# Zero stores of a decode-attention gradient kernel: their source moved from SBUF to memory, and one of them moved in the queue

## The chip, the cores and the metric

The kernel runs on one core of one Trainium2 chip. The metric is the time of one execution on the device in microseconds; lower is better. Before the change it is 282.77 us, the median of 3 runs (282.73 to 283.42).

## What is computed

The reference is a forward pass and its gradients for one decode step. All tensors are bf16.

```python
def _fwd_reference(A_x, A_k_cache, A_v_cache, A_wq, A_wo, B_x, B_w_gate, B_w_up, B_w_down):
    x = A_x                                   # [4, 1, 512]
    xn = _layernorm(x, axis=-1)
    return x + _A_ref(xn, A_k_cache, A_v_cache, A_wq, A_wo) + _B_ref(xn, B_w_gate, B_w_up, B_w_down)
...
# inside _A_ref: only the last W = 1024 of Sk = 4096 cached positions are used
k = jnp.repeat(k_cache[:, :, Sk - W:, :], rep, axis=1)
v = jnp.repeat(v_cache[:, :, Sk - W:, :], rep, axis=1)
...
_out, _vjp = jax.vjp(_f, A_x, A_k_cache, A_v_cache, A_wq, A_wo, B_w_gate, B_w_up, B_w_down)
return (_out, *_vjp(grad_out))
```

`_A_ref` is attention with 32 query heads and 8 key/value heads of width 128; `_B_ref` is a gated feed-forward layer with 1792 hidden columns. The outputs are the result (out_0) and the gradients of x (out_1), of the two caches (out_2 for K, out_3 for V, each 4 x 8 x 4096 x 128), and of the five weights (out_4 to out_8).

For this change one thing matters: the first 3072 of 4096 positions of each cache have no part in the result, so their gradients are zero, and the kernel has to write these zeros. That is three quarters of out_2 and out_3: 50.3 MB.

## The kernel before

All five engines follow an order written out by hand; the program says what each engine issues and in what sequence, and a framework adds the semaphore waits that the data need.

The kernel loads the feed-forward weights first and computes the feed-forward part. Then it goes through the attention in NT = 4 steps of two key/value heads each (`for t in range(NT)`; in the text the steps are also called groups, so the second group is t = 1). In each step K and V blocks are transposed on TensorE, scores and their softmax are formed, and from them the gradients of V and K (`dvdk`), of wo and wq (`dw`), and partial sums for x. The gradient work is cut into pieces of about one matmul and one copy out of PSUM. Pieces are put in a list, `bg`, and `tick(n)` takes the next n of them, so that they fill the gaps of the following work; most pieces of step t thus run while step t + 1 is under way. When the last piece of an output tile is done, the piece stores it. The tiles are named after what they hold: `stg_dv` and `stg_dk` are gradients of V and K (1 MB each), `osb_o` and `osb_q` gradients of wo and wq (512 KB each), `osb_d` and `osb_g` those of the feed-forward weights.

Nearly all transfers are issued from SyncE's queue (SP), in program order: the loads of K and V (`load_kv`, line 133) and all large stores (`store`, line 103). `store` issues an empty instruction that carries the waits, and then the DMA; stores of results are declared free of dependences on each other and on the zero stores, while zero stores are checked against each other.

The zero stores are made by `zero(n)`. A list `zlist` holds 32 regions, each 2 heads x 3072 positions x 128 columns of one batch row, 1.5 MB; regions of out_2 and out_3 alternate. `zero(n)` takes the next n regions and stores a zero tile `ztile` of 128 partitions x 12 KB to each. In memory, each partition's 12 KB become one contiguous row, 128 rows for one store. `zero` is called where the order wants bytes to move: three times in a row at the beginning (line 168), after some stores of the feed-forward gradients, after each store of `stg_dv` or `stg_dk` (in `dvdk`), four times in a row in the last step after the second half of its transposes (`if t == NT - 1: zero(4)`), and for whatever is left at the end.

The list's first region is `out_2[0, 0:2, 0:K0, :]` with K0 = 3072. The store that the change adds a call to is in `piece_q`, the piece for the gradient of wq: each step has two such stores (c2 = 0 and 1), and those of t = 1 are issued while t = 2 is computed.

Of the kernel before, what the change touches and what calls it, by code (L numbers as in the profile page):

```python
# [14 lines left out]
P = 128  # L15
# [3 lines left out]
def kernel(  # L19
# [28 lines left out]
    nc = tc.nc  # L48
# [7 lines left out]
    K0 = Sk - W  # L56
    F = B_w_gate.shape[1]
    ND = D // P
    NF = F // P
    GP = 2  # L60
    NT = G // GP
# [27 lines left out]
    def evac(out, in_, n, half=False, eng=None):  # L89

        eng = "dve" if half else eng
        ca, cd = (190 + n) / 1.2, (120 + (n / 2 if half else n)) / 0.96
        if eng is None:
            eng = "act" if load["act"] + ca <= load["dve"] + cd else "dve"
        load[eng] += ca if eng == "act" else cd
        if eng == "act":
            return nc.scalar.copy(out=out, in_=in_)  # L97
        return nc.vector.tensor_copy(out=out, in_=in_)  # L98

    def store(eng, out, in_, kind):  # L100

        eng.nop()
        d = eng.dma_start(out=out, in_=in_)
        for k in ("rest", "zeros") if kind == "rest" else ("rest",):
            tc.declare_no_dep(d.ins, group=k, reason="stores write disjoint parts of the outputs")
        tc.add_to_no_dep_group(kind, d.ins)
        return d
# [12 lines left out]
    def load_w(t, eng=nc.gpsimd):  # L120
        pool = w_pool[t % 2]
        wo_t[t] = pool.tile([P, HG, D], BF16, name="wo_sb", tag="wo")
        eng.dma_start(out=wo_t[t][:], in_=wo_v[t])
        wq_t[t] = pool.tile([P, ND, CW], BF16, name="wq_sb", tag="wq")
        eng.dma_start(out=wq_t[t][:], in_=wq_v[t])
# [30 lines left out]
    ZR = 2  # L156
    ZW = K0 * Dh * ZR // P
    ztile = const.tile([P, ZW], BF16, name="ztile")
    zlist = deque((og, b, g) for b in range(B) for g in range(0, G, ZR) for og in (out_2, out_3))

    def zero(n=1):
        for _ in range(min(n, len(zlist))):
            og, b, g = zlist.popleft()
            store(nc.sync, og[b, g:g + ZR, 0:K0, :].rearrange("g (m j) d -> m g (j d)", m=P // ZR), ztile[:], "zeros")


    nc.gpsimd.memset(ztile[:], 0.0)
# [94 lines left out]
    def tick(n):  # L262
        for _ in range(min(n, len(bg))):
            bg.popleft()()
# [3 lines left out]
    def link(n=1):  # L268
        for _ in range(min(n, len(chain))):
            chain.popleft()()  # L270
# [227 lines left out]
    def dw(t):  # L498
        o_s, dq_r = st[t]["os"], st[t]["dq"]

        def piece_o(g, i, held):
            if i == 0:
                held["osb"] = outp.tile([P, rep, D], BF16, name="osb_o", tag="o")
            mps = ps_w.tile([P, D], FP32, name="dwo_ps", tag="w")
            nc.tensor.matmul(mps[:], lhsT=o_s[:, g].rearrange("p r d -> p (r d)")[:, i:rep * Dh:rep], rhs=dyr[:],  # L505
                             start=True, stop=True)
            evac(held["osb"][:, i, :], mps[:], 512)
            if i == rep - 1:
                r0 = (t * HG + g * rep) * Dh
                store(nc.sync, out_5[r0:r0 + rep * Dh, :].rearrange("(p i) n -> p (i n)", i=rep),  # L510
                      held["osb"][:].rearrange("p i n -> p (i n)"), "rest")

        def piece_q(c2, k, held):
            if k == 0:
                held["osb"] = outp.tile([P, 2, GP, rep, Dh], BF16, name="osb_q", tag="o")
            ci, i2 = k // 2, k % 2
            c = c2 * 2 + ci
            mps = ps_w.tile([P, 2, GP, Dh], FP32, name="dwq_ps", tag="w")
            for i in range(2):
                nc.tensor.matmul(mps[:, i].rearrange("p g d -> p (g d)"), lhsT=xnm[:, i2 * 2 + i, c * P:(c + 1) * P],  # L520
                                 rhs=dq_r[:].rearrange("p g d -> p (g d)"), start=True, stop=True)
            evac(held["osb"][:, ci, :, i2 * 2:(i2 + 1) * 2, :], mps[:].rearrange("p i g d -> p g i d"), 512)
            if k == 3:
                store(nc.sync, out_4[c2 * 2 * P:(c2 + 1) * 2 * P, t * CW:(t + 1) * CW].rearrange("(c p) j -> p c j", p=P),
                      held["osb"][:].rearrange("p c g i d -> p c (g i d)"), "rest")

        assert rep == 4
        made = []
        for g in range(GP):
            held = {}  # L530
            made.append([lambda g=g, i=i, held=held: piece_o(g, i, held) for i in range(rep)])
        for c2 in range(ND // 2):
            held = {}
            made.append([lambda c2=c2, k=k, held=held: piece_q(c2, k, held) for k in range(4)])
        return made
# [181 lines left out]
    with tc.tile_pool(name="kv_b", bufs=GP, reuse_waits="tile") as kv_b, \  # L717
            tc.tile_pool(name="w_b", bufs=1, reuse_waits="tile") as w_b, \
            tc.tile_pool(name="stage", bufs=3, reuse_waits="tile") as stage:
        kv_pool[1], w_pool[1] = kv_b, w_b  # L720
        zero()
        pre(0)
        load_w(1)
        load_kv(1, 0)
        for t in range(NT):
            kv_steps(t, 0, 0)
            if t == 0:
                zero()
                load_kv(1, 1)
                zero()  # L730
            softmax(t)
            kv_steps(t, 1, 1)
            if t == NT - 1:
                zero(4)
            link(len(chain))
            softmax_d(t)
            link()
            odq(t, 0)
            load_kv(t + 2, 1)
            if t + 1 < NT:  # L740
                pre(t + 1)
            link(len(chain))
            odT(t, 0)
            odq(t, 1)
            load_kv(t + 2, 0)
            tick(2)
            odT(t, 1)
            fin(t)
            if t + 2 < NT:
                load_w(t + 2)  # L750
            (k0, k1), (o0, o1, q0, q1) = dvdk(t, 1), dw(t)
            for p in (k0, o0, k1, o1, q0, q1):
                bg.extend(p)
        tick(len(bg))
        zero(len(zlist))

        fin_ps = []
        for o in range(2):
            f_ps = ps_w.tile([B, ND, P], FP32, name="f_ps", tag="w")
            for c in range(ND):  # L760
                nc.tensor.transpose(f_ps[:, c, :], acc[:, o, c, :], ident_f[:])
            fin_ps.append(f_ps)
        acc_o = fin_ps[0][:].rearrange("b c p -> b (c p)")
        acc_d = attw.tile([B, P, ND], FP32, name="acc_d", tag="P_s")
        nc.vector.tensor_copy(out=acc_d[:].rearrange("b p c -> b c p"), in_=fin_ps[1][:])
        acc_d = acc_d[:].rearrange("b p c -> b (p c)")
        out_b = attw.tile([B, D], BF16, name="out_b", tag="pT")
        nc.vector.tensor_tensor(out=out_b[:], in0=acc_o, in1=x4[:], op=ALU.add)
        nc.scalar.dma_start(out=out_0.rearrange("b s d -> (b s) d"), in_=out_b[:])

        s1 = attw.tile([B, 1], FP32, name="s1", tag="m")
        nc.vector.reduce_sum(out=s1[:], in_=acc_d, axis=AX.X)
        pr = attw.tile([B, D], FP32, name="pr", tag="dS_s")
        s2 = attw.tile([B, 1], FP32, name="s2", tag="es")
        nc.vector.tensor_tensor_reduce(out=pr[:], in0=acc_d, in1=xn_f[:], scale=1.0, scalar=0.0,
                                       op0=ALU.mult, op1=ALU.add, accum_out=s2[:])
        nm1 = attw.tile([B, 1], FP32, name="nm1", tag="rr")
        nc.vector.tensor_scalar(out=nm1[:], in0=s1[:], scalar1=-1.0 / D, scalar2=None, op0=ALU.mult)
        nm2 = attw.tile([B, 1], FP32, name="nm2", tag="gs")
        nc.vector.tensor_scalar(out=nm2[:], in0=s2[:], scalar1=-1.0 / D, scalar2=None, op0=ALU.mult)  # L780
        nc.vector.scalar_tensor_tensor(out=pr[:], in0=xn_f[:], scalar=nm2[:, 0:1], in1=acc_d,
                                       op0=ALU.mult, op1=ALU.add)
        nc.vector.tensor_scalar(out=pr[:], in0=pr[:], scalar1=nm1[:, 0:1], scalar2=rstd[:, 0:1],
                                op0=ALU.add, op1=ALU.mult)
        dx_b = attw.tile([B, D], BF16, name="dx_b", tag="E_f")
        nc.vector.tensor_tensor(out=dx_b[:], in0=pr[:], in1=dy4[:], op=ALU.add)
        nc.scalar.dma_start(out=out_1.rearrange("b s d -> (b s) d"), in_=dx_b[:])
# [30 lines left out]
```

## Time and profile before

| | |
|---|---|
| median of 3 runs | 282.77 us |
| the profiled execution | 283.0 us |
| its span (first to last instruction) | 281.0 us |
| TensorE busy | 203.1 us, 72% |
| VectorE busy | 164.1 us, 58% |
| ScalarE busy | 117.8 us, 42% |
| DMA, mean over the span | 399 GB/s |
| K and V loads, 16 of 1024 KB | 17.4 us (K) and 20.7 us (V) from issue to landing |
| SP waiting at line 103 for zero stores | 14.9 us, 6 times |

The profile is of one execution. Its page cuts the span into 40 slices of 7 us and gives for each how busy an engine or the DMA engines were, in tenths (9 means 90% or more), and how many GB/s moved. The granted clock of TensorE is 0.901 of full speed on average. A row of the table of DMA issues has the tiles, the engine that issued, the count, the size of one, and the median time from issue to landing. In the answers for windows, the columns after the window are its length, the busy microseconds of PE, PEld, DVE, ACT and POOL with the number of instructions, then TensorE's granted clock, the mean busy share of the 16 DMA engines, and GB/s. A packet is counted in the window in which it starts, so that shares a little above 1 occur in short windows. In a timeline of SP, the columns are the start, the duration and the operation; SP's instructions are the issues of DMAs.

### The profile page before, as it was taken

The page shows a single profiled execution, that of the slowest core. Times are in us where ns is not written, and L with a number is a line of the kernel's source. Part 1 is how long each engine was busy: PE and PEld are TensorE (multiplying, and loading weights), DVE is VectorE, ACT ScalarE, POOL GpSimd, SP SyncE. Part 2 cuts the span into 40 slices and gives each one's busy share as a digit, 9 for nine tenths or more (in the row PEclk, how much of TensorE's full clock was granted, in tenths as well). Part 3 has the DMA queues.
Part 4 walks back from the last instruction along what each step waited for, and adds up shares of the span by engine and source line. Part 5 has one row for each costly group of instructions (what it writes and reads, how often), then busy time and mean ns, then how long its engine had stood idle before and what let it go on. Part 6 is the DMA issues. An engine that isn't in the chain of part 4 may idle for free.

```text
span 281.0 us, 6867 instructions
## 1 busy us (share of the span) xinstructions
PE 203.1 (72%) x2972; PEld 138.8 (49%) x2972; DVE 164.1 (58%) x313; ACT 117.8 (42%) x219; POOL 40.1 (14%) x40
## 2 busy tenths in 40 slices
PE   0276699959789889998999299898999599390000
PEld 0265476735456665566775156677556484140000
DVE  7946646645776655577666067767677728386000
ACT  2030386635035418764448056443866038370000
POOL 8600000007002150002250000223000400000000
PEclk9999589986999999999999969999999979977555
DMA  7999999999999999999999999999999999999990
GB/s 264 393 375 431 431 426 417 425 419 424 369 395 424 422 420 420 426 415 422 419 417 411 412 424 423 431 383 398 385 368 415 387 432 410 425 429 422 398 422 30
DMA packets 19565, 112.12 MB, mean 399 GB/s; under 512 B 1664, under 2 KB 4496, under 8 KB 11088
## 3 DMA queue, kind: packets, MB, share of 16 engines
q1 hardware_dynamic: 17744, 103.56, 89.6%
q0 software_dynamic: 1632, 6.29, 5.6%
q10 hardware_dynamic: 160, 1.84, 1.9%
q8 instruction: 23, 0.38, 0.5%
q14 instruction: 6, 0.05, 0.0%
HBM read 30.68 MB, written 81.01 MB: 397 GB/s over the span
## 4 chain that ended last, share of the span: by engine, by line
PE 47%; DMA 22%; DVE 16%; ACT 4%; issue 2%; SPq 0%; DVEq 0%; ACTq 0%
DMA out_dram<-stg_dv 13%; PE T_ps L279 8%; PE kv_ps L484 7%; DMA wd_sb<-in_B_w_down_dram 6%; PE S_ps L345 5%; PE od_ps L450 5%; DMA out_dram<-osb_g 4%; DVE T_sb L98 3%; DVE dS_s L367 2%; PE wdT_ps L279 2%; PE dwq_ps L520 2%; PE acc_ps L256 2%; PE dwd_ps L660 2%; DVE P_s L367 2%; PE wgT_ps L279 2%
## 5 line engine op out<-in xcount | busy, mean ns | idle before, releaser
L98 DVE COPY T_sb<-T_ps 128x1024 bf16<-128x1024 bf16 x64 | 44.1, 688 | 26.7 <-PE T_ps L279 26.5
L97 ACT CAST stg_dk<-kv_ps 128x512 bf16<-128x512 f32 x52 | 29.2, 588 | 31.2 <-PE kv_ps L484 12.4
L97 ACT CAST stg_dv<-kv_ps 128x512 bf16<-128x512 f32 x51 | 28.1, 588 | 24.9 <-PE kv_ps L484 24.3
L484 PE MATMUL kv_ps<-qmr,dS_s 128*128 128x512 bf16 x64 | 23.9, 414 | 11.3 <-ACT stg_dk L97 10.6
L463 POOL TENSOR_TENSOR o_s<-od_r,msk_r 128x512 bf16<-128x512 bf16 x8 | 9.1, 1157 | 110.2 <-DVE od_r L455 80.9
L484 PE MATMUL kv_ps<-domr,P_s 128*128 128x512 bf16 x64 | 21.3, 382 | 0.0
L279 PE MATMUL T_ps<-ident,vb 128*128 128x128 bf16 x256 | 20.3, 225 | 0.4 <-DVE T_sb L98 0.4
L279 PE MATMUL T_ps<-ident,kb 128*128 128x128 bf16 x256 | 20.4, 225 | 0.0
L279 PEld LDWEIGHTS <-kb 128*128 128x128 bf16 x256 | 17.5, 101 | 4.5 <-issue 1.3
L279 PEld LDWEIGHTS <-vb 128*128 128x128 bf16 x256 | 17.2, 101 | 5.0 <-issue 3.2
L97 ACT CAST osb_q<-dwq_ps 128x512 bf16<-128x512 f32 x25 | 14.6, 587 | 8.3 <-PE dwq_ps L520 7.4
L329 POOL TENSOR_TENSOR domr<-r,msk 128x1024 bf16<-128x1024 bf16 x4 | 7.6, 1892 | 71.2 <-DVE r L326 65.1
L97 ACT CAST osb_g<-dwg_ps 128x512 bf16<-128x512 f32 (+1 forms) x25 | 12.3, 544 | 12.3 <-PE dwg_ps L673 6.3
L97 ACT CAST osb_o<-dwo_ps 128x512 bf16<-128x512 f32 x24 | 13.9, 586 | 4.5 <-PE dwo_ps L505 2.9
L98 DVE CAST stg_dk<-kv_ps 128x512 bf16<-128x512 f32 x12 | 8.0, 688 | 12.0 <-DMA out_dram<-stg_dv 11.2
L98 DVE COPY wgT<-wgT_ps 128x1024 bf16<-128x1024 bf16 x14 | 9.6, 686 | 6.8 <-PE wgT_ps L279 6.8
L345 PE MATMUL S_ps<-T_sb,qm 128*32 128x256 bf16 x128 | 12.7, 387 | 0.6 <-DVE T_sb L98 0.5
L345 PE MATMUL S_ps<-T_sb,dom 128*32 128x256 bf16 x128 | 12.7, 388 | 0.1
L505 PE MATMUL dwo_ps<-dyr,o_s 128*128 128x512 bf16 x32 | 12.4, 413 | 0.3 <-ACT stg_dk L97 0.2
L98 DVE COPY woT<-woT_ps 128x1024 bf16<-128x1024 bf16 x16 | 11.0, 686 | 2.7 <-PE woT_ps L279 2.3
L484 PEld LDWEIGHTS <-dS_s 128*128 128x128 bf16 x64 | 6.2, 101 | 12.2 <-issue 11.1
L520 PE MATMUL dwq_ps<-od_r,xnm 128*128 128x256 bf16 x64 | 11.6, 274 | 0.3 <-ACT osb_q L97 0.2
(188 smaller groups left out, 385.0 us busy)
## 6 DMA issues: line engine op xcount, KB each, us to landing
out_dram<-ztile SPq DMA_DIRECT2D x32, 1536.0 KB, 18.1
kb<-in_A_k_cache_dram SPq DMA_DIRECT2D x8, 1024.0 KB, 17.4
vb<-in_A_v_cache_dram SPq DMA_DIRECT2D x8, 1024.0 KB, 20.7
out_dram<-stg_dv SPq DMA_DIRECT2D x8, 1024.0 KB, 13.0
out_dram<-stg_dk SPq DMA_DIRECT2D x8, 1024.0 KB, 20.8
out_dram<-osb_o SPq DMA_DIRECT2D x8, 512.0 KB, 17.4
out_dram<-osb_q SPq DMA_DIRECT2D x8, 512.0 KB, 13.8
out_dram<-osb_g SPq DMA_DIRECT2D x8, 448.0 KB, 14.3
```

The costliest lines, as they stand in the source:

```text
L97: return nc.scalar.copy(out=out, in_=in_)
L98: return nc.vector.tensor_copy(out=out, in_=in_)
L256: nc.tensor.matmul(ps[:, c, :], lhsT=lf(c), rhs=rhs, start=(k == 0), stop=(k == len(terms) - 1))
L279: nc.tensor.transpose(ps[:, i, :], a, ident[:])
L329: nc.gpsimd.tensor_tensor(out=mr[:].rearrange("p g q d -> p (g q) d"), in0=r4[:, k, :].unsqueeze(1).broadcast_to([P, SL, Dh]), in1=msk[:]. ...
L345: nc.tensor.matmul(ps[b * RB:(b + 1) * RB, :], lhsT=zt[:, b * GP + g, c0:c0 + RB], rhs=T_sb[:].rearrange("p (x b) -> p b x", b=B)[:, b, :] ...
L367: nc.vector.scalar_tensor_tensor(out=out[:], in0=src[:].unsqueeze(2).broadcast_to([P, WQ, B]), scalar=rr[:, 0:1], in1=mskb[:].unsqueeze(1) ...
L450: nc.tensor.matmul(od_ps[g * 32:g * 32 + B * rep, k, g, :], lhsT=cols[:, jj, g * NQ + q, :], rhs=blks[(t, g)][:, j, :], start=(j == 0), st ...
L463: nc.gpsimd.tensor_tensor(out=o_s[:, g], in0=rows[:, g].unsqueeze(1).broadcast_to([P, rep, Dh]), in1=msk_r[:].unsqueeze(2).broadcast_to([P ...
L484: nc.tensor.matmul(mps[:].rearrange("p q d -> p (q d)"), lhsT=src[:, j * P:(j + 1) * P], rhs=mr[:, g].rearrange("p q d -> p (q d)"), start ...
L505: nc.tensor.matmul(mps[:], lhsT=o_s[:, g].rearrange("p r d -> p (r d)")[:, i:rep * Dh:rep], rhs=dyr[:], start=True, stop=True)
L520: nc.tensor.matmul(mps[:, i].rearrange("p g d -> p (g d)"), lhsT=xnm[:, i2 * 2 + i, c * P:(c + 1) * P], rhs=dq_r[:].rearrange("p g d -> p ...
```

## The change

Three lines of behaviour change.

- The first three zero stores still copy `ztile`. The other 29 copy the first region, which the first zero store has written, from memory to memory. Both sides are viewed in rows of 24 KB, 64 rows for one store.
- One call of `zero` is added behind the second store of the gradient of wq of the second group (t = NT - 3 = 1, c2 = 1).
- In the last step `zero(4)` becomes `zero(3)`. The total stays 32 stores, and the order of regions is the same.

```diff
     zlist = deque((og, b, g) for b in range(B) for g in range(0, G, ZR) for og in (out_2, out_3))
+    ZN = len(zlist)
 
     def zero(n=1):
+
         for _ in range(min(n, len(zlist))):
             og, b, g = zlist.popleft()
-            store(nc.sync, og[b, g:g + ZR, 0:K0, :].rearrange("g (m j) d -> m g (j d)", m=P // ZR), ztile[:], "zeros")
+            dst = og[b, g:g + ZR, 0:K0, :]
+            if len(zlist) >= ZN - 3:
+                store(nc.sync, dst.rearrange("g (m j) d -> m g (j d)", m=P // ZR), ztile[:], "zeros")
+            else:
+                store(nc.sync, *(x.rearrange("g (m j) d -> m g (j d)", m=32) for x in (dst, out_2[0, 0:ZR, 0:K0, :])), "zeros")
...
             if k == 3:
                 store(nc.sync, out_4[c2 * 2 * P:(c2 + 1) * 2 * P, t * CW:(t + 1) * CW].rearrange("(c p) j -> p c j", p=P),
                       held["osb"][:].rearrange("p c g i d -> p c (g i d)"), "rest")
+                zero(t == NT - 3 and c2 == ND // 2 - 1)
...
             if t == NT - 1:
-                zero(4)
+                zero(3)
```

## The prediction, made before the change was run

> **What bounds the kernel now.** I read the forty slices of the page first, then its DMA queues and its table of DMA issues.
>
> ```profile
> span 281.0 us, 6867 instructions
> ...
> DMA  7999999999999999999999999999999999999990
> GB/s 264 393 375 431 431 426 417 425 419 424 369 395 424 422 420 420 426 415 422 419 417 411 412 424 423 431 383 398 385 368 415 387 432 410 425 429 422 398 422 30
> DMA packets 19565, 112.12 MB, mean 399 GB/s; under 512 B 1664, under 2 KB 4496, under 8 KB 11088
> ...
> q1 hardware_dynamic: 17744, 103.56, 89.6%
> ...
> HBM read 30.68 MB, written 81.01 MB: 397 GB/s over the span
> ...
> out_dram<-ztile SPq DMA_DIRECT2D x32, 1536.0 KB, 18.1
> ```
>
> The 16 DMA engines are 90% or more busy in 38 of 40 slices, while TensorE has 72% of the span and VectorE 58%. So the **bytes through the DMA engines** set the time. The zero stores are 32 x 1.573 MB = 50.3 MB of the 112.1 MB. The chain of waits hides this: it walks back from VectorE's last operation at 257.2 us, though bytes are moved until 276 us.
>
> Next the three-microsecond windows in which almost only zeros move, and the two-microsecond windows in which the DMA share drops:
>
> ```profile
> 33.00:36.00 3.00, 1.47 (x9) 0.96 (x10) 1.27 (x2) 1.99 (x4) 0.00 (x0) 0.50 1.02 434
> 225.00:228.00 3.00, 3.00 (x64) 2.89 (x60) 0.00 (x0) 0.00 (x0) 0.00 (x0) 0.53 0.96 403
> 228.00:231.00 3.00, 3.00 (x58) 2.23 (x55) 1.09 (x5) 1.92 (x4) 0.00 (x0) 0.90 1.08 444
> ...
> 186.00:188.00 2.00, 1.92 (x37) 1.20 (x38) 1.45 (x6) 1.54 (x4) 0.00 (x0) 1.00 0.78 309
> 194.00:196.00 2.00, 1.36 (x37) 1.27 (x38) 0.96 (x3) 0.00 (x0) 0.00 (x0) 1.00 0.87 352
> 200.00:202.00 2.00, 2.00 (x25) 1.14 (x22) 1.19 (x3) 1.69 (x3) 0.00 (x0) 1.00 0.73 307
> 210.00:212.00 2.00, 1.89 (x21) 1.25 (x18) 1.17 (x5) 1.78 (x5) 0.00 (x0) 1.00 0.71 291
> ```
>
> The last two columns are the DMA share and GB/s. In the first group the zero stores run at 403 to 444, about 427 GB/s together, out of SBUF. In the second the engines stand partly idle. The queue's own instructions show why:
>
> ```profile
> 174.87 3.01 SPq L103 DMA_DIRECT2D out_dram<-osb_q  x2
> 186.84 0.55 SPq L103 DMA_DIRECT2D out_dram<-stg_dv  x1
> ...
> 219.74 4.40 SPq L103 DMA_DIRECT2D out_dram<-ztile  x4
> 233.63 0.54 SPq L103 DMA_DIRECT2D out_dram<-stg_dv  x1
> ```
>
> SP issues nothing from 177.9 to 186.8 us, and the engines run dry. From 224.1 to 233.6 it issues nothing either, but the four zero stores cover that gap.
>
> From the trace's packet records: 4 KB, 8 KB and 12 KB packets take 159, 309 and 460 ns (medians), that is 150 ns for 4096 bytes (27.2 GB/s on each engine) and some 9 ns for a packet. The mean of 12 KB packets is 467 ns. Only zero stores have 12 KB packets (4096 of them), so the records also tell how many of the 16 engines are in a zero store at any moment. Missing engines sum to 2.3 us of all 16 between 186 and 222 us (0.4, 0.2, 0.7, 0.7, 0.3 at 186, 194, 200-203, 208-211, 218-221).
>
> [...]
>
> **The change, part by part.**
>
> 1. *Larger rows.* 29 stores have 64 packets of 24 KB instead of 128 of 12 KB. A 24 KB packet, extended at the same slope: 460 + 3 x 150 = about 912 ns, against 2 x 460 = 920. Each engine has four such pairs in a store, so 4 x 8 x 29 = **-0.9 us**, all on the path, as the engines are full. On SP, the same number of instructions is issued.
>
> 2. *Source in memory.* 29 x 1.573 = 45.6 MB are now also read from memory[...]. The engine's own rate has no reason to rise above 27.2 GB/s: it is the rate of loads and stores alike. What rises is the traffic at memory: 16 engines in zero stores read 435 and write 435 GB/s, 870 together, where the trace never showed over 455. No row of this trace prices it. From below: memory takes 870, cost 0 (and the mean excess of 467 - 460 ns, 7 x 8 x 29 = 1.6 us, may be regained if it came from SBUF: down to -1.6). From above: a ceiling C. With the first three stores left out, the packet records have 10 or more engines in zero stores for 89.5 us, with 13.86 on average; the demand there is 27.2 x (16 + 13.86) = 812 GB/s. [...] The same sum over the records gives [...]22.8 at 650, 34.3 at 600 (if changing between reads and writes costs something), 3.6 at 800. I take 14.0[...]. Engines that drift further apart would mix zero copies with other transfers and bring it down; the records show such drift already (between 110 and 120 us 5 to 8 engines are in zero stores at a time, rarely all). By stages the 14.0 are 2.6 up to 80 us, 1.6 to 180, 2.2 to 222, 3.3 to 238, 4.3 after.
>
> 3. *The wait for the first store.* Every copy reads what the first store writes. That store was issued at 18.5 us; the first 128 of the 12 KB packets had started by 35.4 us, while the first copy comes at 40.8 us, so it is over or nearly. If not, SP holds for some us with the d-weight stores queued behind it (the next comes at 42.6 us), while the two other zero stores still fill the engines until 44 us: 0. If each copy waited for the copy before it, SP would hold up all later loads and stores; nothing in the slices of before, where zero stores follow each other too, speaks for that.
>
> 4. *The moved store.* It leaves the run of four at 219.7 and is issued at about 178 us, one DMA, with SP idle until 186.8: no one is queued behind it. 1.573 MB at 427 GB/s are 3.7 us of work, more than the 2.3 us of holes that follow. On an otherwise unchanged queue this gains up to 2.3. But the run it leaves covers the gap to 233.6: the first d-value packets start at about 235.9, so some 2.3 us lay ahead of them then, and part of the gain (I put 1.4, the rest of the time a DMA takes to begin) opens a new hole there. Alone: **-0.9 to -2.3**. With part 2 the copies run late, so neither the old holes nor the new one remain: **-2.3**, whichever part fills them.
>
> Sum: 281.0 - 0.9 + 14.0 - 2.3 = 291.8 us span. The profiled execution took 283.0, 2.0 more than its span: 293.8. It is 0.2 above the median of 282.77, so **293.6 us**.
>
> **Rivals.**
>
> *Faster: memory takes it.* If reads and writes together pass at over 870 GB/s, or the engines drift apart so far that the demand stays under the ceiling, parts 1, 4 and perhaps 1.6 us of part 2 remain: -0.9 - (0.9 to 2.3) - (0 to 1.6), thus 278.0 to 281.0 us, 280.0 at the middle. It decides from where the excess is less than about 3.2 us: by the sums above, a ceiling of 805 GB/s or more. For it: nothing in this trace shows a ceiling on memory.[...]
>
> *Within 0.3%.* A ceiling that drift mostly hides (excess of 2 to 4 us) would be cancelled by parts 1 and 4: 282 to 283.6.
>
> *Much slower: turning between reads and writes.* At 600 GB/s, 281.0 - 3.2 + 34.3 + 1.8 = about 314 us. At worst reads and writes of a copy take turns, and each takes twice its 3.7 us: 29 x 3.7 = 107 more, 387 us.
>
> *The change doesn't do what it says:* were the copies cut into small packets, the DMA table would show many more packets; rows of 24 KB are contiguous on both sides, so I give it nothing apart from the case above.
>
> **How the numbers follow.** Slower through the ceiling 0.64 (of it 0.12 above 306, at the 600 end), taking turns 0.03, cancelled 0.08, faster 0.25. About 0.3% (0.85 us) is what a measurement can tell from no change. Slower is then 0.67, same 0.08, faster 0.25. The range begins at 279.5, which leaves out some 0.05 below, and ends at 306, which leaves out 0.15: that is a ceiling of about 640. The slower case alone: 284 to 314.
>
> **What would show it.** Right: packets of 24 KB whose mean is well over 912 ns[...], windows of pure zero copies near 350 GB/s on the DMA line instead of 427, memory read at about 76 MB on the page, no drop of the DMA share at 186 to 212 us, the largest loss after 222 us. Wrong: 24 KB packets at 912 ns and windows of 430 GB/s; then the time falls below 282. If SP waits on the zero stores more than before (14.9 us in its waits), part 3 was wrong.

## The result and the profile after

The changed kernel takes 292.68 us (median of 4 runs, 291.68 to 292.95) against 282.88 us, a ratio of 1.0336 with a 95% interval of 1.0308 to 1.0364: **9.8 us slower**. The forecast was 293.6 us. The profiled execution took 291.68 us, with a span of 289.7 us, 8.7 more than before.

From the page of the kernel after, the slices and the DMA queues:

```profile
span 289.7 us, 6866 instructions
...
DMA  7999999999999999999999999999999999998793
GB/s 266 393 383 429 431 417 424 378 412 386 343 416 407 415 383 422 421 429 419 411 411 415 421 440 427 413 409 400 382 353 364 394 344 369 417 421 346 304 348 115
DMA packets 17709, 112.12 MB, mean 387 GB/s; under 512 B 1664, under 2 KB 4496, under 8 KB 11088
...
q1 hardware_dynamic: 15888, 103.56, 90.4%
...
HBM read 76.29 MB, written 81.01 MB: 543 GB/s over the span
```

Packets fell by 1856 and 45.6 MB more are read, as the diff says. The engines are nearly as busy as before, but they move less: slices of 344 and 348 GB/s stand where almost only copies move (232 to 239 us and 275 to 282 us). The two slices between 261 and 275 us (346 and 304) hold a gap as well, which is taken up under "The last stores". Windows of the kernel after show the copies closer; the columns are those of before:

```profile
228.00:238.00 10.00, 9.12 (x150) 7.23 (x151) 4.20 (x12) 3.99 (x8) 1.07 (x1) 0.83 1.00 350
274.00:284.00 10.00, 0.00 (x0) 0.00 (x0) 0.00 (x0) 0.00 (x0) 0.00 (x0) 0.50 1.05 347
```

A share of 1.00 with 350 GB/s, where zero stores from SBUF had 403 to 444, means that each packet holds its engine for longer. The records of single packets in the trace say by how much. The 24 KB packets take 912 ns in the median, the undisturbed time that the prediction extended from smaller packets, but 998 ns in the mean, and the time depends on how many of the 16 engines copy together (the mean number over the packet's time, rounded; odd numbers are left out):

```
engines that copy at the same time   mean of a 24 KB packet   read + written by these engines
 8                                     934 ns                    421 GB/s
10                                     964 ns                    510 GB/s
12                                    1055 ns                    559 GB/s
14                                    1062 ns                    648 GB/s
16                                    1108 ns                    710 GB/s
```

(The last column is 24576 bytes x 2 x engines / mean. The other engines move some 25 GB/s each beside them, 8 KB in 323 ns, so at 10 to 16 the total is about 660 to 710. These are means. Summed over the packet records in the same way, this kernel holds at most 692 GB/s over 10 us, but 793 over 3 us and 816 over 2 us.)

The sum of all packet times, divided by 16 engines, is 274.6 us before and 284.6 after: 10.0 us more. That is 10.0 us for the copies above 912 ns (1856 x 86 / 16) and 2.7 for other packets (8 KB ones 323 ns instead of 317), less 2.6 because two 12 KB packets had taken 2 x 467 ns. This sum is a mean over the 16 engines, and that it comes close to the 9.8 us is partly chance: between the two profiled executions the span grew by 8.7 us, and, as shown below, it is the last engine that sets the span.

### The profile page after: what moved, and what is told of

Same layout as the page of the kernel before. It is cut to its first block, busy times and chain, and to the rows that moved or that the text cites. A ratio compares the mean times of both kernels' runs of the same rounds, so it can differ in the third digit from the quotient of the medians.

```text
span 289.7 us, 6866 instructions
## 1 busy us (share of the span) xinstructions
PE 205.7 (71%) x2972; PEld 141.2 (49%) x2972; DVE 164.3 (57%) x313; ACT 117.8 (41%) x219; POOL 40.1 (14%) x40
## 3 DMA queue, kind: packets, MB, share of 16 engines
HBM read 76.29 MB, written 81.01 MB: 543 GB/s over the span
## 4 chain that ended last, share of the span: by engine, by line
DMA 47%; PE 29%; DVE 9%; ACT 4%; issue 2%; SPq 1%; ACTq 0%; DVEq 0%
DMA out_dram<-stg_dv 21%; DMA out_dram<-osb_o 9%; DMA wd_sb<-in_B_w_down_dram 5%; PE kv_ps L490 5%; DMA out_dram<-osb_d 4%; DMA out_dram<-osb_g 4%; PE T_ps L285 4%; PE od_ps L456 4%; DMA out_dram<-out_dram 3%; PE S_ps L351 3%; PE wdT_ps L285 2%; PE woT_ps L285 2%; ACT osb_d L97 1%; PE dwq_ps L526 1%; DVE T_sb L98 1%
## 5 line engine op out<-in xcount | busy, mean ns | idle before, releaser
L490 PE MATMUL kv_ps<-domr,P_s 128*128 128x512 bf16 x64 | 22.3, 397 | 1.9 <-DVE woT L98 1.8
L285 PE MATMUL T_ps<-ident,kb 128*128 128x128 bf16 x256 | 19.5, 219 | 0.4 <-ACT osb_g L97 0.4
L285 PEld LDWEIGHTS <-kb 128*128 128x128 bf16 x256 | 16.6, 98 | 4.9 <-issue 1.7
L285 PE MATMUL woT_ps<-ident,wo_sb 128*128 128x128 bf16 x128 | 12.0, 248 | 2.1 <-ACT osb_g L97 2.0
L351 PE MATMUL S_ps<-T_sb,qm 128*32 128x256 bf16 x128 | 12.7, 386 | 0.6 <-DVE T_sb L98 0.5
L351 PE MATMUL S_ps<-T_sb,dom 128*32 128x256 bf16 x128 | 12.7, 387 | 0.1
```

Of the source, the lines that this page charges most:

```text
L285: nc.tensor.transpose(ps[:, i, :], a, ident[:])
L351: nc.tensor.matmul(ps[b * RB:(b + 1) * RB, :], lhsT=zt[:, b * GP + g, c0:c0 + RB], rhs=T_sb[:].rearrange("p (x b) -> p b x", b=B)[:, b, :] ...
L490: nc.tensor.matmul(mps[:].rearrange("p q d -> p (q d)"), lhsT=src[:, j * P:(j + 1) * P], rhs=mr[:, g].rearrange("p q d -> p (q d)"), start ...
```

## The experiments

**The move alone.** The kernel before, with the two lines of the move and no copies.

```diff
+                zero(t == NT - 3 and c2 == ND // 2 - 1)
...
-                zero(4)
+                zero(3)
```

> The kernel before with only the zero store moved behind the second group's last dwq store; all zero stores still copy the zero tile from SBUF. Theory (memory is the ceiling, the copies are the whole loss): the holes of 2.3 us between 186 and 222 us are filled, up to 1.4 us may open after 224 us; 280.5 to 282.0 us against 282.9, ratio 0.992 to 0.997. Rival (the move costs: the run of three no longer covers the wait for the next gradient of V): 283 to 285 us.

Measured: 283.40 us, ratio 1.0012 (1.0001 to 1.0024). This is neither: the move gains nothing and loses next to nothing. From the windows of this kernel, first around the next store of a V gradient, then at the end:

```profile
232.00:234.00 2.00, 1.99 (x21) 1.28 (x20) 1.65 (x4) 2.00 (x4) 0.00 (x0) 1.00 0.81 344
234.00:236.00 2.00, 1.94 (x37) 1.25 (x36) 1.42 (x4) 1.02 (x3) 0.00 (x0) 1.00 0.55 225
...
272.00:274.00 2.00, 0.00 (x0) 0.00 (x0) 0.00 (x0) 0.00 (x0) 0.00 (x0) 0.50 0.53 224
274.00:276.00 2.00, 0.00 (x0) 0.00 (x0) 0.00 (x0) 0.00 (x0) 0.00 (x0) 0.50 0.07 31
276.00:278.00 2.00, 0.00 (x0) 0.00 (x0) 0.00 (x0) 0.00 (x0) 0.00 (x0) 0.50 0.06 25
278.00:280.00 2.00, 0.00 (x0) 0.00 (x0) 0.00 (x0) 0.00 (x0) 0.00 (x0) 0.50 0.04 18
```

The new hole of 1.3 us at 232 to 236 is the one that the prediction had priced at 1.4. But the last lines hold what it had overlooked. From 274 us on, the DMA share is 0.06, one engine in sixteen. The kernel before ends in the same way:

```profile
274.00:276.00 2.00, 0.00 (x0) 0.00 (x0) 0.00 (x0) 0.00 (x0) 0.00 (x0) 0.50 0.15 61
276.00:278.00 2.00, 0.00 (x0) 0.00 (x0) 0.00 (x0) 0.00 (x0) 0.00 (x0) 0.50 0.06 25
278.00:280.00 2.00, 0.00 (x0) 0.00 (x0) 0.00 (x0) 0.00 (x0) 0.00 (x0) 0.50 0.04 18
```

**One engine ends last and sets the time.** The trace has 16 increments of the semaphore for each large store, as many as there are engines. Read as one from each engine, the records of these increments show how far the last engine is behind the median one. In the kernel before it is 5.5 us behind at 185 us, 6.8 us at 198 us, and 5.4 us at the end (279.9 against 274.5 us). With the move alone, the median engine ends at 273.4 us, 1.1 us earlier, and the last one at 280.0 us, as before. So the holes seem to have been those of the other engines, and to have cost nothing. The next experiment tests this.

**One store more.** The kernel before, with a 33rd zero store where the change moves one.

```diff
+                if t == NT - 3 and c2 == ND // 2 - 1:
+                    zlist.appendleft((out_2, 0, 0))
+                    zero()
```

> The kernel before, which keeps its run of four, with a 33rd zero store from SBUF (the first region once more) at the place to which the change moves one, about 178 us. Theory (the end is set by one DMA engine some 6 us behind the others, which never runs dry between 186 and 222 us; the holes are those of the other engines): the store costs its whole 3.7 us, 286.5 to 287.2 us. Rival (the holes of 2.3 us are on the path): it costs 3.7 - 2.3 = 1.4 us, 284.3 to 285 us.

Measured: 286.75 us, ratio 1.0126 (1.011 to 1.0142), 3.6 us more by this ratio and 3.3 by the medians. The theory of the late engine had said 3.7, that of the holes 1.4. The windows of this kernel show that the holes were filled all the same (0.78, 0.87, 0.73 and 0.71 before):

```profile
186.00:188.00 2.00, 1.92 (x49) 1.47 (x50) 1.53 (x7) 0.95 (x3) 0.43 (x1) 1.00 1.07 431
194.00:196.00 2.00, 1.75 (x40) 1.52 (x41) 0.81 (x3) 0.18 (x1) 0.00 (x0) 1.00 1.05 444
200.00:202.00 2.00, 2.00 (x27) 1.14 (x24) 1.37 (x3) 1.18 (x3) 0.00 (x0) 1.00 1.02 430
210.00:212.00 2.00, 1.89 (x26) 1.51 (x24) 1.40 (x3) 1.33 (x4) 0.00 (x0) 1.00 0.98 410
```

And by the increments the median engine ends at 274.6 us, as before, since it had room; the last ends at 283.6, 3.7 us later than before.

**Zeros alone.** All other work is left out: three stretches of zero stores with nothing beside them, in one execution.

```diff
+    for kind, n in (("sbuf", 10), ("copy", 12), ("half", 10)):
+        for _ in range(n):
+            zero(kind)
...
+            for h in range(ZR):
+                put(*(x[h].rearrange("(q m j) d -> m q (j d)", m=8, q=4) for x in (dst, src)))
```

(The last two lines are the third stretch, with 8 rows outermost, so that 8 engines share a copy.)

> Zero stores by themselves, all the rest of the computation left out: 10 from the zero tile, then 12 copies of 1.5 MB on all 16 engines, then 20 copies of 0.75 MB laid out so that 8 engines share each. Theory (ceiling): 12 KB packets at 460 ns and about 427 GB/s in the first part; 24 KB packets at about 1110 ns and 355 GB/s in the second; 24 KB packets near 912 ns and 215 GB/s in the third, where reads and writes sum to 430. Rival (a copy from memory is slow on each engine): third part at about 1100 ns and 178 GB/s.

The three stretches as windows of this kernel; its only busy engine column is POOL, then come the clock, the DMA share and GB/s:

```profile
10.00:40.00 30.00, 0.00 (x0) 1.00 1.01 426
55.00:100.00 45.00, 0.00 (x0) 1.00 1.00 322
105.00:170.00 65.00, 0.00 (x0) 1.00 0.50 215
```

Stores from SBUF move 426 GB/s, copies by 16 engines 322, and copies by 8 engines 215. With 8 engines, every packet after 105 us takes 912 ns; with 16, the mean is 1194 ns. A copy isn't slow on its engine; 16 of them together are. Nor are some of the 16 slow and the others not: the last copy of the second stretch ends on 15 engines between 102.3 and 103.7 us and on the last at 104.8. The 322 GB/s copied are 644 read and written, less than the expected 710 and less than the best mixture in the kernel. So the sum of reads and writes is a fair measure, but not a fixed limit: at about 660 together a packet takes 964 ns where 10 engines copy in the kernel, and it takes 1194 ns at 644 here. Where the engines meet, in the memory itself or on the way to it, and whether the addresses of 16 copies side by side matter, no run separates; "memory" below stands for all of these.

**The copies without the move.**

```diff
-                zero(t == NT - 3 and c2 == ND // 2 - 1)
...
-                zero(3)
+                zero(4)
```

> The changed kernel without the move: 29 copies from memory, four zero stores in a row as before. Theory (ceiling): the copies run late, so the holes between 186 and 222 us are mostly gone without the move, and the move is worth under 1 us here: 292 to 294 us. Rival (the move is worth its full 2.3 us beside the copies too): 295 us or more, with the holes of 2 us in the DMA share back. In both, the last stores wait for the semaphores of the two small outputs, as in the changed kernel.

Measured: 295.74 us, ratio 1.0445 (1.0428 to 1.0463). So the rival was right on the number: the copies alone cost 12.6 us, and beside them the move is worth 3.1 us. The gap before the next V gradient is still there in the windows of this kernel:

```profile
188.00:192.00 4.00, 4.00 (x65) 2.95 (x62) 2.26 (x5) 1.86 (x4) 0.00 (x0) 0.75 0.76 302
192.00:196.00 4.00, 3.92 (x96) 2.87 (x95) 2.18 (x8) 1.92 (x5) 2.36 (x2) 1.00 0.82 291
```

But the reason isn't the hole alone. The packet time is 288.0 us here, 3.4 more than in the changed kernel; 24 KB packets take 1015 ns. Of the copies' packets, 608 find 15 or 16 engines copying, in the changed kernel 398. After the hole the median engine is within 0.1 to 0.5 us of the first until 228 us, where it was 3.4 us behind it before: waiting for the same store has put the engines in step. That this crowds the copies is a reading and not tested alone; in the changed kernel the distance shrinks as well, but later (3.0 us at 195 us, 0.4 to 0.6 from 204 us to 227 us).

**Which part of the move gains.** To tell that apart, this run is the changed kernel with its run of four kept; the moved copy is then taken from those at the very end.

```diff
-                zero(3)
+                zero(4)
```

> The changed kernel with its run of four copies kept (zero(4)), so that the copy issued at about 178 us is taken from the two at the very end. With copies, the move was worth 3.1 us (295.7 without, 292.7 with it). Theory A (filling the gap before 191 us keeps the engines from falling into step, so that fewer copies coincide afterwards): the gain stays, 292.3 to 293.3 us. Theory B (three copies in a row instead of four is what gains): it is lost, 295 to 296 us.

Measured: 294.39 us (292.49 to 295.31), ratio 1.0381 (1.0354 to 1.0407), between the two. Filling the gap seems to give a part of the 3.1 us and the shorter run the rest, but the runs are too wide apart to divide it. This stays open.

**Half of the copies.**

```diff
-            if len(zlist) >= ZN - 3:
+            if len(zlist) >= ZN - 3 or og is out_3:
```

> The changed kernel with only the zero stores to out_2 as copies from memory (14); those to out_3 are from the zero tile in SBUF again. Copies and stores from SBUF alternate. Theory (a ceiling of memory that only a crowd of copies reaches): engines a few us apart hardly ever copy all at once, so far less than half of the 9.8 us is lost: 283 to 286 us. Rival (each copy costs its own surplus, however many there are): 14/29 of 9.8 us, 4.7 us: 287.6 us.

Measured: 286.38 us, ratio 1.0101 (1.0076 to 1.0127): 2.9 to 3.2 us for 14 of 29 copies, a third of the loss. This lies between the theories, 0.4 us above the range of the one and 1.2 us under the rival. Alternation does not keep the copies apart: the 24 KB packets average 1006 ns, no less than the 998 with all 29, and in 36 us there are still 10 or more engines in a copy, because, as it seems, most engines reach the same store within its 3.7 us (in the kernel before, most large stores from 170 us on end on the median engine 0.1 to 2.2 us after the first). The packet time is 5.2 us over the kernel before, half of the 10.0: in packet time each copy does cost its own surplus, as the rival had it. Not all of it reaches the end, and the increments of the last store show where it goes. The median engine ends 4.4 us later than in the kernel before (278.9 us), the last engine only 2.7 us later (282.6 us), and the profiled span is longer by the same 2.7. Why the last engine loses less than the others isn't settled.

**Another source.**

```diff
-                ... for x in (dst, out_2[0, 0:ZR, 0:K0, :])), "zeros")
+                ... for x in (dst, A_k_cache[b, g:g + ZR, 0:K0, :])), "zeros")
```

> The changed kernel with each of the 29 copies reading its own region of the K cache (so the gradient regions hold K values instead of zeros, and no copy depends on the first store). Theory (the sum of reads and writes is the limit): 292 to 293.5 us as the changed kernel, 24 KB packets at about 1100 ns where all 16 engines copy. Rival (one hot region of 1.5 MB is read again and again, or the wait for the first store holds the copies): well under, 283 to 289 us.

Measured: 292.29 us, ratio 1.032 (1.0284 to 1.0357); 1137 ns where all 16 engines copy. So neither one region that is read again and again nor the wait for the first store is the cause.

**Rows of 12 KB.**

```diff
-                ... rearrange("g (m j) d -> m g (j d)", m=32) ...
+                ... rearrange("g (m j) d -> m g (j d)", m=64) ...
```

> The changed kernel with its copies in rows of 12 KB (128 packets for a copy, as the stores from SBUF have) instead of 24 KB. Theory: the rows are worth 0.9 us, at the ceiling even less: 292.7 to 293.8 us. Rival (long rows are what makes the copies slow): 290 us or less.

Measured: 292.38 us, ratio 1.0319 (1.0288 to 1.035), the same as with 24 KB. All zero packets together take 126.5 us per engine here and 126.9 in the changed kernel. Half as many packets of twice the size gained nothing here.

**The last stores.** In the changed kernel SP waits long at its end. From SP's waits between 245 and 290 us:

```profile
SPq L103 <- DMA out_dram<-out_b: 6.8, 1, 6.8
...
SPq L103 <- DMA out_dram<-dx_b: 5.9, 1, 5.9
```

and its timeline and the DMA share there:

```profile
256.62 0.59 SPq L103 DMA_DIRECT2D out_dram<-stg_dk  x1
264.06 0.57 SPq L103 DMA_DIRECT2D out_dram<-out_dram  x1
270.58 0.35 SPq L103 DMA_DIRECT2D out_dram<-osb_o  x1
```

```profile
262.00:264.00 2.00, 0.00 (x0) 0.00 (x0) 1.93 (x7) 0.00 (x0) 0.00 (x0) 0.73 0.78 328
264.00:266.00 2.00, 0.00 (x0) 0.00 (x0) 0.93 (x2) 0.00 (x0) 0.00 (x0) 0.50 0.84 301
268.00:270.00 2.00, 0.00 (x0) 0.00 (x0) 0.00 (x0) 0.00 (x0) 0.00 (x0) 0.50 0.79 309
270.00:272.00 2.00, 0.00 (x0) 0.00 (x0) 0.00 (x0) 0.00 (x0) 0.00 (x0) 0.50 0.42 172
```

The framework gives the DMAs of SP and ScalarE eight semaphores in turn (the increments in the trace carry eight numbers, 100 to 104 and 108 to 110), and a DMA of SP waits until the one before it on its semaphore has landed: in the changed kernel out_0 lands on 110 at 264.0 us and out_1 on 100 at 270.5 us, and the next DMAs on these numbers are issued at 264.1 and 270.6 us. With the copies it hands the small outputs out_0 and out_1 other numbers than before: two of SP's last six stores now share theirs, the copy at 264.1 us and the store of `osb_o` at 270.6 us, and wait for two outputs that are computed last of all. In the kernel before, the same two waits fall two stores and more later and are shorter (3.6 and 2.0 us). With the move alone SP issues its last stores as before (from 259.7 and 262.9 us, before from 259.5 and 263.3); with the copies alone it stands from 259.9 to 269.7 us, so the copies change the numbers and not the move. The next run is the kernel after with these two issued from GpSimd:

```diff
-        nc.scalar.dma_start(out=out_0.rearrange("b s d -> (b s) d"), in_=out_b[:])
+        nc.gpsimd.dma_start(out=out_0.rearrange("b s d -> (b s) d"), in_=out_b[:])
...
-        nc.scalar.dma_start(out=out_1.rearrange("b s d -> (b s) d"), in_=dx_b[:])
+        nc.gpsimd.dma_start(out=out_1.rearrange("b s d -> (b s) d"), in_=dx_b[:])
```

> The changed kernel with the two small outputs (out_0, out_1) issued from GpSimd instead of ScalarE, so that they use other semaphores and no store of SP waits for them. Theory of the tail (in the changed kernel SP stands from 256.6 to 264.1 and on to 270.6 us until the small outputs have landed, and the engines lose 2.4 us between 262 and 272): 2 to 2.5 us less than the changed kernel, about 290 us, and no drop of the DMA share there. Rival (the engines would have been held by the memory ceiling anyway): within 0.5 us of the changed kernel, about 292.5 us.

Measured: 291.48 us, ratio 1.0296 (1.0273 to 1.032). The hole is gone, as windows of this kernel show:

```profile
262.00:266.00 4.00, 0.00 (x0) 0.00 (x0) 3.46 (x9) 0.00 (x0) 0.70 (x2) 0.91 1.05 445
266.00:270.00 4.00, 0.00 (x0) 0.00 (x0) 0.00 (x0) 0.00 (x0) 0.38 (x1) 0.50 0.98 405
270.00:272.00 2.00, 0.00 (x0) 0.00 (x0) 0.00 (x0) 0.00 (x0) 0.00 (x0) 0.50 1.08 432
```

but only about 1.2 of the 2.4 us that the engines lost there came back, with intervals that overlap: between the theories. The increments of the last store tell why it isn't more:

```
us in the profiled execution            median engine ends   last engine ends
kernel before                            274.5                279.9
the move alone                           273.4                280.0
one store more                           274.6                283.6
kernel after                             285.7                288.6
kernel after, out_0, out_1 on GpSimd     281.1                287.6
```

Without the hole the median engine ends 4.6 us earlier, but the last one, which has more left to do, only 1.0. It is the finding of the first two experiments once more: the hole was mostly that of the other engines.

> The kernel before with the zero store moved and the two small outputs issued from GpSimd; all zero stores from SBUF. Theory: with zeros from SBUF the last stores wait for the small outputs later and the engines never ran dry there, so this equals the kernel with the move alone within 0.5 us: 280.5 to 282.0 us. Rival (the waits for the small outputs cost in the kernel before too): 279 to 280.5 us, a us or more under the move alone.

This is the move alone with the same edit. Measured: 283.59 us, ratio 1.0017 (1.0006 to 1.0027), as without the edit (1.0012). With zeros from SBUF these waits cost nothing that can be measured: the last engine ends at 280.0 us with the edit and without it. No version is faster than the kernel before.

## Why the prediction was right, and where it was not

The time was right within 1 us, and so was the main mechanism, but two steps were wrong and one was missing. That the total came so close is partly luck: the copies were forecast at +13.1 us with their rows and cost 12.6 alone, part of it through waits that the forecast did not have, and the move was forecast at -2.3 beside them and gave -3.1, for another reason than the one given.

*What bounds the kernel*: right that the bytes through the DMA engines do, but incomplete. The last of the engines does, not their mean; the chain of waits and the DMA share of whole slices don't show it, the last windows do. With the change the median engine ends 11.2 us later and the last one 8.7 us later, so a sum over the mean of the engines, like the one for the ceiling, can be off by some us.

*Part 1, larger rows, -0.9 us*: failed. It took the engine's time for a packet as the price, though part 2 makes memory the price while many engines copy. Measured: with rows of 12 KB the zero packets take 0.4 us less per engine, not 0.9 more, and the times don't differ (1.0319 against 1.0336, each known to about 0.003, so that they alone would not settle 0.9 us).

*Part 2, the source, +14.0 us*: right in kind. Measured, the copies take 10.0 us more than undisturbed ones and the other packets 2.7 more, 12.7 together. Against the mean of the stores that they replaced, which was above the undisturbed time too, 2.6 us came back; the prediction had left 1.6 of this as possible and put the rest under part 1. The ceiling behind the 14.0 us was assumed: no trace of before shows one, and the sums of the prediction, each the time by which the demand of the engines exceeds a ceiling, say how much hangs on it (3.6 us at 800 GB/s, 34.3 at 600). Measured, reads and writes together are 660 to 710 GB/s in the kernel where 10 to 16 engines copy, and 644 with nothing but copies. Of the marks set down, the 24 KB packets (998 ns in the mean, and 1108 where all 16 engines copy), the windows (350 and 347) and the memory read (76.29 MB) hold; the DMA share between 186 and 212 us no longer falls under 0.90; and the largest loss lies after 222 us. The time of the copies above 912 ns, by the forecast's five stages, is 1.8, 0.5, 1.6, 2.3 and 3.8 us, where 2.6, 1.6, 2.2, 3.3 and 4.3 had been forecast: the course is right, the size too large by some 4 us.

*Part 3, the wait for the first store, 0*: right. The first copy is issued at 41.0 us, where the store of before was at 40.8, and with a source that needs no wait the time is the same. The mark that was to show this part wrong did appear: SP's waits for zero stores at line 103 rose from 14.9 to 21.0 us. But all of these are for later copies and none is for the first store, so it was the mark that was badly chosen.

*Part 4, the move, -0.9 to -2.3 alone, and -2.3 beside the copies "whichever part fills them"*: failed twice. Alone it gives 0 (1.0012), because the sum averaged idle time over 16 engines, while the last one ends no earlier when it is filled. Beside the copies the lag does not fill the holes by itself: without the move they remain (0.76 and 0.82). The move is worth 3.1 us there, so the -2.3 came near by luck; less crowding of the copies is the likely reason, not a shown one.

*Missing*: the waits of the last stores for the two small outputs, about 1.2 us (the intervals overlap).

The rival "faster" fell because memory did not take 870 GB/s in the changed kernel. Its point of decision, 805, was passed there over 2 us (816) but no longer over 3 us (793); with nothing beside them, the copies held 755 over their first 5 us.

## What to carry to other kernels

A copy from memory to memory uses the memory twice (the page's reads rose from 30.68 to 76.29 MB here, with the same 81.01 MB written): before it replaces a store from SBUF, sum reads and writes over the engines that will do it at the same time, and reckon with 640 to 710 GB/s for all together, as these runs had it (644 with nothing but copies, 660 to 710 beside other transfers). Before filling a hole in the DMA share, look at the end of the trace: if the share falls to one sixteenth there (0.06 from 276 to 278 us in the kernel before), one engine is late, and a hole of the others need not cost anything (filling the holes gave a ratio of 1.0012). And a change that shifts the rotation of DMA semaphores can make early stores wait for late ones (6.8 and 5.9 us here, where it had been 3.6 and 2.0), so read SP's waits after every such change.

## What the runs showed that was not expected

One DMA engine of sixteen runs behind the median in the kernels with zeros from SBUF: 4.7 to 7.0 us in the kernel before between 176 us and the end, and 9.0 us at the end with one store more; what it does more than the others was not found. A candidate is the fetching of instructions, on the page's instruction queue 23 packets of 16 KB, 966 ns each in the mean, in the kernel before: rises of the lag by 1.3 to 1.4 us at 18, 101 and 107 us fall together with such a packet, but the records don't say on which engine a packet ran. With the copies but not the move, engines that ran dry together came out in step (the median 0.1 to 0.5 us behind the first, instead of 3.4), and then seem to crowd the memory together (608 packets with 15 or 16 engines copying, against 398). Among the zeros alone, eight engines copy at 215 GB/s with no loss (912 ns a packet), sixteen at 322 (1194 ns). And the crowd of copies began faster there than it went on: the first 5 us hold 755 GB/s of reads and writes, the whole stretch 644 (in windows, 388 GB/s are copied from 45 to 50 us, 344 from 50 to 55, and 322 from 55 to 100).
